# GpSimd's waits for the VectorE operation planned ahead of it, taken out of a retention and SwiGLU kernel

## The chip, the core and the metric

The kernel runs on one core of a Trainium2 chip. The metric is the device time of one execution in microseconds (us); of several executions the median counts. The engines are TensorE (PE, with its weight loads as PEld), VectorE (DVE), ScalarE (ACT), GpSimd (POOL) and SyncE (SP), which issues nearly all DMAs.

## What is computed

A retention layer (linear attention with a decay per head) over 4 sequences of 768 positions and 8 heads of 64, in blocks of 64, and behind it an RMS norm and a SwiGLU layer with 512 inputs and 1536 hidden columns:

```python
for b in range(nb):                       # retention, block by block
    intra = einsum('bhic,bhjc->bhij', qb, kb) * Dmask
    intra = einsum('bhij,bhjd->bhid', intra, vb)
    inter = einsum('bhid,bhde->bhie', qb * lam_pow, kv_state)
    out[:, :, sl] = intra + inter
    kv_state = lam_block * kv_state + einsum('bhsd,bhse->bhde', kb * rev_pow, vb)
...
xn = x / sqrt(mean(x * x) + 1e-06) * rms_g   # x: the layer's rows, 3072 x 512
g, val = xn @ w_gate, xn @ w_val
return (silu(g) * val) @ w_out
```

## The kernel before

The 3072 rows are worked on in 6 groups of 512 (m), the hidden columns in 12 blocks of 128 (f). A unit is a group and a block: gate and value products, SiLU, their product. Each float32 operand is split into a high and a low float16 part, and a product is made of three float16 products. The first 24 units (groups 0 and 1) use the weights as they are (`classical`, matmuls at L668 with 512 columns). The others use a scheme of seven half-size products in place of eight (`strassen`, L779 with 256 columns), which needs sums of blocks of the weights and of the rows. The retention of a later group is done between units, a pair of heads at a time (`Pair`): scores (L477), the decayed scores (`decay_a`, L497), the states (L510, L523, L525), the mix (L538, L549), squares for the norm (L572, added up at L578, and over the partitions at L589). The rows of the result are made at L938 for group 0 and at L1050 for the others.

GpSimd does 102 tensor operations: the decay of q (`decay_q`, L501), sums of squares (`add_squares`, L578), the power for the norm (`root`, L612), low parts of the normed rows (L644), of their sums (`low_sums`, L663) and of the weights' sums (`low`, L729), and the sum of a weight's high and low part (`whole`, L708). VectorE does the same kinds of work on other tiles, and besides: conversion of the weights' bits (L216, L219), their low parts (L440), sums of the weights (L717 to L721) and of the output weights (L269 to L275), the unit's sums and products (L837, L845, L857, L866), the low parts of the operands of the last product (L922, L1013).

The order of the work is made by a planner (`Plan`). Each step has an engine, a cost, a due time, what it reads and writes and the buffers it opens; `Plan.run` (L1154) simulates the engines and sets the order. `SHIFTS`, a table, moves due times of single steps. The planner holds that GpSimd and some VectorE steps exclude each other: `shared(i)` (L1150) is true for every GpSimd step and for the VectorE steps named in `SHARED` (L1096), and `run` lets neither start before the other's last one is 0.13 us from its end (L1191, L1237).

The loop behind `order = plan.run()` (L1958) writes the steps down in the planned order. Each engine carries out its own instructions in that order, and waits on semaphores where data or buffers ask for it. The planned turn between the two engines is no such reason. So the loop adds one: after a shared VectorE step, the next GpSimd step gets a wait for that step's last instruction. VectorE gets no wait for GpSimd.

Of the kernel before, what the change touches and what calls it, by code (L numbers as in the profile page):

```python
# [22 lines left out]
def retention_swiglu_kernel(  # L23
# [11 lines left out]
    nc = tc.nc  # L35
# [1221 lines left out]
    plan = Plan()  # L1257
# [241 lines left out]
    def arrive_steps():  # L1499
        def arrive():  # L1500
            pass

        step("LD", 4.3, -9, arrive, w=["cs", "come"])
        times = [0.75, 1.3, 1.55, 1.35, 1.85, 1.3, 1.3, 1.3]
        for p in range(NP):
            for i, c in enumerate(("qK", "kv")):
                step("LD", times[2 * p + i], -9, arrive, w=["come", *[f"q0_{p}:{x}" for x in c]])
        step("LD", 3.05, -9, arrive, w=["come", "gv0"])

    def ramp_steps():  # L1510
        pm = []

        def largest_of_all():
            pm.append(scales())

        def make_scales():
            scales_of(pm[0])

        step("DVE", 0.13, -3.1, largest, r=["cs"], w=["gmax"])
        step("PE", 0.3, -3.1, largest_of_all, r=["gmax"], w=["pmax"], new=[("pmax", "g")])  # L1520
        step("DVE", 1.33, -2.35, make_scales, r=["pmax"], w=["gs"])
        for p in range(NP):
            for part in range(3):
                w = f"pw{p}" if part == 2 else f"mask{2 * p + part}"
                step("DVE", 0.38, -3.2 + 0.4 * p + 0.15 * (part == 2), powers, p, part, r=["cs"] + ["wv11"] * (part == 2), w=[w])
        ats = [-2.85, -2.3, -2.0, -1.75]
        pairs = [Pair(0, p) for p in range(NP)]
        for q, at in zip(pairs, ats):
            pair_scores(q, at)
            pair_sums(q, at + 0.4)  # L1530
            pair_mix(q, at + 0.5)
        first_norm_steps(0, -0.3, 0.05)
        for p, at in enumerate(ATTENTION_1):
            q = Pair(1, p)
            pair_scores(q, at)
            pair_sums(q, at + 0.5)
            pair_mix(q, at + 0.6)
        first_norm_steps(1, 5.0, 0.05)
        for f, at in enumerate(CONVERT):
            wt = Weights(f)  # L1540
            if wt.halves:
                for i in range(2):
                    halved_steps(wt, at + 0.2 * i, i)
            else:
                convert_steps(wt, at)
                split_steps(wt, at + 0.35)
# [196 lines left out]
    def load_steps():  # L1743
        queue = [(1, 0), (1, 1), (1, 2), 1, (1, 3), *range(2, NF)]
        queue += [(m, p) for m in range(2, NG) for p in range(NP)]
        for n, key in enumerate(queue):
            cost = 2.65 if n < 5 else 3.0 if n < 10 else 3.6
            lasts = (0.1, 0.1, 0.5, 0.4)[n] if n < 4 else 2.3
            if isinstance(key, tuple):
                m, p = key  # L1750
                if key == (3, 1):
                    step("LD", 0.0, -9, operand_tiles, new=[("tx0", "in"), ("tx1", "in")],
                         w=[f"{t}:{o}{i}" for t in ("tx0", "tx1") for o in "hl" for i in range(2)]
                         + [f"vals{i}:{j}" for i in range(2) for j in range(2)])
                name = f"q{m}_{p}"
                step("LD", cost, -9, load_qkv, m, p, w=[f"{name}:{c}" for c in "qKkv"], new=[(name, "in")], lasts=lasts)
            else:
                step("LD", cost, -9, load_gv, key, w=[f"gv{key}"], new=[(f"gv{key}", "in")], lasts=lasts)
# [123 lines left out]
    with tc.manual_schedule(  # L1882
        engines={
            mybir.EngineType.PE, mybir.EngineType.DVE, mybir.EngineType.Activation,
            mybir.EngineType.Pool, mybir.EngineType.SP,
        }
    ):
        hs = {u: Hidden(u, m, f) for u, (m, f) in enumerate(units)}
        columns = {u: [] for u in range(2 * NF)}
        arrive_steps()  # L1890
        load_steps()
        ramp_steps()
        out_weights = [out_weight_steps(j, at) for j, at in enumerate(OUT_W)]
        end = len(units)
        pair = None
        for u in range(end):
            for f in COLUMNS.get(u, []):
                columns[u + 1].append(column_steps(f, u - 0.7))
            if u == FACTORS:
                factor_steps(u)  # L1900
            for f in range(NF):
                if int(SUMS[f]) == u:
                    sum_steps(f, SUMS[f])
            h = hs[u]
            m, f = h.m, h.f
            if u < 2 * NF:
                classical(u, h, columns[u])
                n = u - (2 * NF - 8)
                if 0 <= n < NP:
                    q = Pair(2, n)  # L1910
                    pair_scores(q, u + 0.62)
                    pair_sums(q, u + 0.64)
                    if pair:
                        pair_mix(pair, u + 0.63)
                    pair = q
                elif n == NP:
                    pair_mix(pair, u + 0.63)
                elif n == NP + 1:
                    norm_steps(2, u, 0.11)
                if u == 2 * NF - 1:  # L1920
                    pair = Pair(3, 0)
                    pair_scores(pair, u + 0.62)
            else:
                strassen(u, h)
                p = (f + 1) // 2 % HALF
                following = m + 2 if f == NF - 1 else m + 1
                if f % 2 == 0 and pair:
                    pair_sums(pair, u + 0.12)
                    pair_mix(pair, u + 0.3)
                    pair = None  # L1930
                if f % 2 and p < NP and following < NG:
                    pair = Pair(following, p)
                    pair_scores(pair, u + 0.1)
                if f == 2 * NP - 1 and m + 1 < NG:
                    norm_steps(m + 1, u, 0.2)
        if PLAIN:
            step("ROOM", 0.0, START[0] - 3, early_room, new=[("early", "big0")], w=["early:"])
        for m in range(PLAIN):
            for j in range(HALF):
                block_steps(m, j, START[m] - 1.5 - 0.3 * (HALF - 1 - j), 0.1)  # L1940
            plain_rows_steps(m, START[m], PLAIN_LENGTH)
        for o, at in zip(out_weights, OUT_SUMS):
            out_sum_steps(o, at)
        for i in range(2):
            room_step(i, START[PLAIN] - 3)
        for m, at in enumerate(START):
            if m < PLAIN:
                continue
            for j in range(HALF):
                t = at - AHEAD[j]  # L1950
                if m == NG - 1:
                    t = units.index((NG - 1, 2 * j + 1)) + 0.5
                operand_steps(m, j, t, 0.1)
            rows_steps(m, at, LENGTH)
        for i, by in SHIFTS.items():
            eng, cost, at, *rest = plan.steps[i]
            plan.steps[i] = (eng, cost, at + by, *rest)
        order = plan.run()  # L1958
        now, gaps = 1.5, True
        traced, ahead = nc.cur_bb.bb.instructions, None  # L1960
        for t, i in order:
            eng, cost, _, fn, args, _, _, new, _ = plan.steps[i]
            begun = len(traced)
            if eng == "PE":
                if any(name.startswith("pb") for name, _ in new):
                    gaps = False
                idle = t - now
                if gaps and idle > 0.8:
                    busy(int((idle - 0.5) / 0.24))
                now = t + cost  # L1970
            fn(*args)
            if plan.shared(i):

                engine = mybir.EngineType.Pool if eng == "POOL" else mybir.EngineType.DVE
                mine = [x for x in traced[begun:] if x.engine == engine]
                if eng == "DVE":
                    ahead = mine[-1].name
                elif ahead:
                    tc.add_manual_dep(
                        mine[0], ahead,  # L1980
                        mybir.DependencyInfo(mybir.DependencyClass.Sync, mybir.DependencyReason.DATA),
                        reason="shared port",
                    )
                    ahead = None

# [63 lines left out]
```

## Time and profile before

| | |
|---|---|
| median of 3 runs | 629.96 us (629.2 to 631.78) |
| the profiled execution | 629.99 us |
| its span, first to last instruction | 628.2 us |
| granted TensorE clock | 1.000 of full speed |
| busy: PE, DVE, ACT, POOL | 622.2, 452.8, 383.9, 127.6 us |
| GpSimd instructions | 113 |

A row of the profile names a line of the kernel, an engine, an operation, what it writes and reads, and times. The end of a matmul is modelled, so that TensorE's busy time says less than the pace of its matmuls. Idle time of an engine is put down to what released the instruction behind it; of several waits that is the one that came last.

### The profile page before, as it was taken

The page shows a single profiled execution, that of the slowest core. Times are in us where ns is not written, and L with a number is a line of the kernel's source. Part 1 is how long each engine was busy: PE and PEld are TensorE (multiplying, and loading weights), DVE is VectorE, ACT ScalarE, POOL GpSimd, SP SyncE. Part 2 cuts the span into 40 slices and gives each one's busy share as a digit, 9 for nine tenths or more (in the row PEclk, how much of TensorE's full clock was granted, in tenths as well). Part 3 has the DMA queues.
Part 4 walks back from the last instruction along what each step waited for, and adds up shares of the span by engine and source line. Part 5 has one row for each costly group of instructions (what it writes and reads, how often), then busy time and mean ns, then how long its engine had stood idle before and what let it go on. Part 6 is the DMA issues. An engine that isn't in the chain of part 4 may idle for free.

```text
span 628.2 us, 14174 instructions
## 1 busy us (share of the span) xinstructions
PE 622.2 (99%) x5665; PEld 479.3 (76%) x5665; DVE 452.8 (72%) x886; ACT 383.9 (61%) x724; POOL 127.6 (20%) x113
## 2 busy tenths in 40 slices
PE   9999999999999999999999999999999999999997
PEld 8864444455657777668888888888889888888886
DVE  6889888777787778788875789634874778546641
ACT  3779799986546764568764685534853564445531
POOL 3531201142825665410020110011000110000000
DMA  8899898888646788878878667744675667343401
GB/s 320 305 318 299 313 313 290 288 279 290 231 148 226 258 284 273 275 265 284 269 268 297 216 212 225 244 179 152 226 224 179 202 207 248 109 135 105 148 18 51
DMA packets 56033, 144.05 MB, mean 229 GB/s; under 512 B 5920, under 2 KB 18208, under 8 KB 54560
## 3 DMA queue, kind: packets, MB, share of 16 engines
q1 hardware_dynamic: 55824, 142.64, 67.3%
q8 instruction: 44, 0.72, 0.5%
q10 hardware_dynamic: 144, 0.52, 0.3%
q14 instruction: 21, 0.17, 0.1%
HBM read 106.96 MB, written 36.18 MB: 228 GB/s over the span
## 4 chain that ended last, share of the span: by engine, by line
PE 94%; DMA 2%; DVE 1%; ACT 1%; SPq 0%; issue 0%; POOL 0%; ACTq 0%; POOLq 0%
PE o L1050 20%; PE pa L779 20%; PE pb L779 15%; PE pv L668 9%; PE pg L668 9%; PE o L938 5%; PE pa L477 4%; PE po L538 3%; PE po L549 3%; DMA qkv<-in_qkv_dram 2%; PE o_own L1050 2%; PE pst L510 2%; PE pss L589 1%; PE unread L144 1%; PE pr L630 0%
## 5 line engine op out<-in xcount | busy, mean ns | idle before, releaser
L779 PEld LDWEIGHTS <-gw 128*128 128x128 f16 x1440 | 139.5, 98 | 21.9 <-issue 0.8
L1050 PE MATMUL o<-wo,late 128*128 128x256 f16 x1152 | 143.9, 273 | 0.5 <-ACT late L1061 0.5
L1050 PEld LDWEIGHTS <-late 128*128 128x128 f16 x1260 | 123.0, 98 | 15.1 <-issue 0.8
L668 PEld LDWEIGHTS <-w_half 128*128 128x128 f16 x576 | 53.9, 98 | 60.5 <-issue 1.5
L833 ACT COPY tx<-pa 128x256 f32<-128x256 f32 x96 | 35.3, 371 | 72.9 <-PE pa L779 55.5
L779 PE MATMUL pa<-tx,gw 128*128 128x256 f16 x576 | 77.4, 273 | 0.0
L668 PE MATMUL pv<-x,w_half 128*128 128x512 f16 x288 | 69.2, 379 | 0.2
L668 PE MATMUL pg<-x,w_half 128*128 128x512 f16 x288 | 66.8, 379 | 0.0
L837 DVE TENSOR_TENSOR tx<-pb,tx 128x256 f32<-128x256 f32 x96 | 40.0, 420 | 31.4 <-PE pb L779 29.1
L779 PEld LDWEIGHTS <-gv 128*128 128x128 f16 x576 | 56.0, 98 | 7.4 <-issue 0.2
L501 POOL TENSOR_TENSOR qkv<-qkv,pw 128x512 f32<-128x512 f32 x24 | 30.6, 1275 | 74.8 <-PE pa L477 66.5
L845 DVE TENSOR_TENSOR sg<-pb,sg 128x256 f32<-128x256 f32 x48 | 20.1, 422 | 35.4 <-ACT sg L841 30.7
L1013 DVE TENSOR_TENSOR late<-s,late 128x1024 f16<-128x1024 f32 x30 | 37.3, 1253 | 5.2 <-ACT late L1009 5.1
L708 POOL TENSOR_TENSOR r<-w_half 128x512 f32<-128x512 f16 x24 | 27.7, 1163 | 63.3 <-DVE w_half L440 25.5
L497 DVE TENSOR_TENSOR a<-pa,mask 128x512 f32<-128x512 f32 x48 | 31.4, 683 | 12.0 <-PE pa L477 8.5
L779 PE MATMUL pa<-x,gv 128*128 128x256 f16 x288 | 39.3, 273 | 0.0
L779 PE MATMUL pb<-x,gv 128*128 128x256 f16 x288 | 39.3, 273 | 0.0
L779 PE MATMUL pa<-x,gw 128*128 128x256 f16 x288 | 39.0, 273 | 0.0
L779 PE MATMUL pb<-tx,gw 128*128 128x256 f16 x288 | 39.0, 273 | 0.0
L779 PE MATMUL pb<-x,gw 128*128 128x256 f16 x288 | 38.7, 273 | 0.0
L938 PE MATMUL o<-wo,early 128*128 128x512 f16 x144 | 34.9, 379 | 0.0
L729 POOL TENSOR_TENSOR ws<-ws,ws 128x512 f16<-128x512 f32 x24 | 28.8, 1210 | 29.3 <-DVE en L325 15.3
(152 smaller groups left out, 1031.0 us busy)
## 6 DMA issues: line engine op xcount, KB each, us to landing
gw<-gw_kept SPq DMA_DIRECT2D x48, 640.0 KB, 4.8
qkv<-in_qkv_dram SPq DMA_DIRECT2D x47, 512.0 KB, 6.0
h<-h_kept SPq DMA_DIRECT2D x30, 512.0 KB, 4.1
h_kept<-sg SPq DMA_DIRECT2D x48, 256.0 KB, 3.4
gv<-gw_kept SPq DMA_DIRECT2D x48, 256.0 KB, 4.4
raw_gv<-in_weights_dram SPq DMA_DIRECT2D x11, 1024.0 KB, 7.2
raw_o<-in_weights_dram SPq DMA_DIRECT2D x24, 256.0 KB, 4.4
gw_kept<-ws SPq DMA_DIRECT2D x12, 512.0 KB, 4.2
```

The lines of the kernel that those rows point to most:

```text
L477: nc.tensor.matmul(self.pa[j][:, c, :], self.kT[r, c, :], self.qT[r, c, :], start=True, stop=True,)
L497: nc.vector.tensor_mul(self.a[:, j], self.pa[j], decay)
L501: eng.tensor_mul(self.qT, self.qT, pw[:, p : p + 1, :].broadcast_to([P, GC, P]))
L668: nc.tensor.matmul(ps, w[:, kk, :], x[:, kk, :], start=i == kk == 0, stop=i == 2 and kk == NK - 1,)
L708: nc.gpsimd.tensor_add(self.r[:, i], w[:, 0], w[:, 1])
L729: eng.tensor_sub(self.to[:, c, 1], self.t[:, c], self.to[:, c, 0])
L779: nc.tensor.matmul(ps, w(ow, k), x(ox, k), start=first and i == k == 0, stop=i == 2 and k == 1, skip_group_check=True,)
L833: nc.scalar.copy(self.val_sums[:, self.half(t)], self.pa)
L837: nc.vector.tensor_add(v, self.pb, v)
L938: nc.tensor.matmul(self.banks[t], h[:, oh, t * P : (t + 1) * P], wo[:, j, 3 + 2 * k : 5 + 2 * k, ow], start=j == k == i == 0, stop=j == HA ...
L1013: eng.tensor_sub(lo, of, hi)
L1050: nc.tensor.matmul(bank[:, t], ops[:, oh, t * P : (t + 1) * P], w[:, ow], start=n in (1, 2, 5) and q == i == 0 and (t == 0 or bank is own) ...
```

## The change

The loop no longer adds the waits. The planner is as it was, so the order of every engine's instructions is the same.

```diff
         now, gaps = 1.5, True
-        traced, ahead = nc.cur_bb.bb.instructions, None
         for t, i in order:
             eng, cost, _, fn, args, _, _, new, _ = plan.steps[i]
-            begun = len(traced)
...
             fn(*args)
-            if plan.shared(i):
-
-                engine = mybir.EngineType.Pool if eng == "POOL" else mybir.EngineType.DVE
-                mine = [x for x in traced[begun:] if x.engine == engine]
-                if eng == "DVE":
-                    ahead = mine[-1].name
-                elif ahead:
-                    tc.add_manual_dep(
-                        mine[0], ahead,
-                        mybir.DependencyInfo(mybir.DependencyClass.Sync, mybir.DependencyReason.DATA),
-                        reason="shared port",
-                    )
-                    ahead = None
```

No instruction moves. What differs are GpSimd's waits, here around 229 us of the profile: the sums of the high and low parts of weights 10 and 11 (`r`, two halves each, L708), the low parts of the sums of weight 8 (`ws_8`, L729) and the power for the norm of group 3 (`y`). The numbers in names are those of buffers; DVE_49, PE_49 and so on are the engines' semaphores.

```order
 L708 TENSOR_TENSOR r_2892<-w_half_96 128x512 [waits DVE_49,Pool_49]
 L729 TENSOR_TENSOR ws_8_2894<-ws_2863,ws_8_2894 128x2x256 [waits DMAHW4_49,DMAHW6_49,DMAHW0_49,Activation_49]
-L729 TENSOR_TENSOR ws_8_2894<-ws_2863,ws_8_2894 128x2x256 [waits DVE_49]
-L708 TENSOR_TENSOR r_2892<-w_half_96 128x512 [waits DVE_49]
-L708 TENSOR_TENSOR r_2960<-w_half_96 128x512 [waits PE_49]
-L708 TENSOR_TENSOR r_2960<-w_half_96 128x512 [waits DVE_49]
+L729 TENSOR_TENSOR ws_8_2894<-ws_2863,ws_8_2894 128x2x256
+L708 TENSOR_TENSOR r_2892<-w_half_96 128x512
+L708 TENSOR_TENSOR r_2960<-w_half_96 128x512 [waits DVE_49,PE_49]
+L708 TENSOR_TENSOR r_2960<-w_half_96 128x512
 L612 TENSOR_TENSOR y_3012<-ms_2969,power 128x4 [waits DVE_49]
```

Three operations in a row lose their wait for VectorE; the first of `r_2960` now names VectorE because the wait that held it implicitly, that of the operation ahead of it, is gone.

## Rows read from the trace of the kernel before

**Rows 1.** The page: busy time of each engine, and the shares of the chain of work that ended last.
```profile
PE 622.2 (99%) x5665; PEld 479.3 (76%) x5665; DVE 452.8 (72%) x886; ACT 383.9 (61%) x724; POOL 127.6 (20%) x113
PE 94%; DMA 2%; DVE 1%; ACT 1%; SPq 0%; issue 0%; POOL 0%; ACTq 0%; POOLq 0%
```
**Rows 2.** Who waited for whom, TensorE alone, all entries: us in total, times, longest us.
```profile
PE unread L144 <- POOL ident masks.py:199: 1.5, 1, 1.5
PE pss L589 <- POOL sq L578: 0.5, 1, 0.5
PE o L1050 <- ACT late L1061: 0.5, 1, 0.5
```
**Rows 3.** The chain that ended last, in order of time: start us, us, what.
```profile
50.49 1.13 DVE w L219
52.34 1.04 PE pv L668 x4
...
114.15 6.91 PE pg L668 x32
...
358.61 5.24 PE o L1050 x48
```
**Rows 4.** Who waited for whom, GpSimd, four entries: us in total, times, longest us.
```profile
POOL tx L663 <- DVE t L275: 5.8, 1, 5.8
...
POOL tx L663 <- DVE ws L721: 4.4, 1, 4.4
...
POOL sq L578 <- DVE ws L721: 3.4, 1, 3.4
...
POOL qkv L501 <- DVE pw L158: 2.8, 1, 2.8
```
**Rows 5.** Instructions in order of time, VectorE around 213 us: start us, us, engine, line, operation, out<-in, shapes, count, [idle before <- what ended it]. Rows of one shape are merged with their count.
```profile
213.25 0.42 DVE L720 TENSOR_TENSOR ws<-r,ws 128x256 f32<-128x256 f32 x1
213.71 1.26 DVE L721 TENSOR_TENSOR ws<-r,ws 128x256 f32<-128x256 f32 x1
215.08 1.29 DVE L497 TENSOR_TENSOR a<-pa,mask 128x512 f32<-128x512 f32 x2
```
**Rows 6.** The same view of GpSimd.
```profile
213.37 1.32 POOL L708 TENSOR_TENSOR r<-w_half 128x512 f32<-128x512 f16 x1 [0.76 <-DVE ws L718]
215.05 1.15 POOL L708 TENSOR_TENSOR r<-w_half 128x512 f32<-128x512 f16 x1 [0.36 <-DVE ws L721]
```
**Rows 7.** The same view around 60 us, GpSimd and VectorE.
```profile
60.32 1.50 POOL L612 TENSOR_TENSOR y<-ms,power 128x4 f32<-128x4 f32 x1 [11.38 <-DVE sc L430]
...
61.09 0.69 DVE L216 TENSOR_SCALAR w<-w 128x1024 int32<-128x1024 int32 x1 [0.72 <-ACT w L209]
```
**Rows 8.** The same view around 40 us: GpSimd, ScalarE, VectorE, TensorE.
```profile
40.82 1.27 POOL L578 TENSOR_TENSOR sq<-sq,sq 128x512 f32<-128x512 f32 x1 [4.38 <-DVE e L426]
...
39.18 0.60 ACT L572 ACTIVATE sq<-po 128x512 f32<-128x512 f32 x1
...
41.34 0.61 ACT L416 ACTIVATE junk<-w 128x512 bf16<-128x512 f32 x1
...
39.51 0.42 DVE L216 TENSOR_SCALAR w<-w 128x512 int32<-128x512 int32 x1
39.96 0.69 DVE L219 SCALAR_TENSOR_TENSOR w<-raw_gv,w 128x512 int32<-128x512 int32 x1
...
42.10 0.16 PE L420 MATMUL pn<-ssq,ones_b 128*128 128x1 bf16 x1
```
**Rows 9.** The same view around 47 us: TensorE, GpSimd, VectorE.
```profile
44.97 1.16 PE L477 MATMUL pa<-qkv 64*128 64x128 f32 x16
...
47.66 1.28 POOL L501 TENSOR_TENSOR qkv<-qkv,pw 128x512 f32<-128x512 f32 x1 [4.34 <-DVE w_half L440]
...
46.78 0.75 DVE L440 SCALAR_TENSOR_TENSOR w_half<-w,sc,w_half 128x512 f16<-128x512 f32 x1 [0.75 <-ACT w_half L436]
...
48.05 1.44 DVE L219 SCALAR_TENSOR_TENSOR wo_f<-raw_o,wo_f 128x512 int32<-128x512 int32 x1
```
**Rows 10.** The same view around 230 us: GpSimd, VectorE, TensorE.
```profile
228.70 1.16 POOL L729 TENSOR_TENSOR ws<-ws,ws 128x512 f16<-128x512 f32 x1 [0.63 <-DVE sg L857]
231.00 2.26 POOL L708 TENSOR_TENSOR r<-w_half 128x512 f32<-128x512 f16 x2 [1.14 <-DVE sq L578]
...
230.22 0.69 DVE L578 TENSOR_TENSOR sq<-sq,sq 128x512 f32<-128x512 f32 x1 [0.76 <-POOL ws L729]
...
231.03 1.00 PE L589 MATMUL pss<-ones,sq 128*128 128x1 f32 x8
```
**Rows 11.** The same view around 355 us: ScalarE, GpSimd, VectorE, TensorE.
```profile
353.52 0.83 ACT L659 CAST tx<-xt 128x768 f16<-128x768 f32 x1 [0.53 <-DVE xt L655]
...
355.42 1.64 POOL L663 TENSOR_TENSOR tx<-xt,tx 128x768 f16<-128x768 f32 x1 [5.30 <-DVE sg L857]
...
354.53 0.75 DVE L857 SCALAR_TENSOR_TENSOR sg<-tx,cg,sg 128x512 f32<-128x512 f32 x1
355.19 0.68 DVE L497 TENSOR_TENSOR a<-pa,mask 128x512 f32<-128x512 f32 x1
...
357.09 0.42 DVE L845 TENSOR_TENSOR sg<-pb,sg 128x256 f32<-128x256 f32 x1 [0.56 <-ACT sg L841]
...
357.80 0.71 PE L779 MATMUL pb<-x,gw 128*128 128x256 f16 x5
```

## The prediction

> **What bounds the kernel now.** The page comes first: TensorE is busy for 622.2 us of a span of 628.2 us, and the chain that ended last lies on it for 94% [rows 1]. Because ends of matmuls are modelled, the chain is read next for their pace: 32 matmuls of 512 columns take 6.91 us, 216 ns each, and 48 of 256 columns take 5.24 us, 109 ns each [rows 3]. They follow one another with nothing between. The table of TensorE's waits has three entries of 2.5 us together, and only one of them, 0.5 us, is a wait for GpSimd [rows 2]. So the change can win little, since TensorE has almost nothing to give back. It can lose: any operation that VectorE delivers later than TensorE needs it adds to the end.
>
> The last view to read is how GpSimd and VectorE treat each other. Around 213 us, VectorE's L720 and L721 have the same shape and both inputs in SBUF. L720 takes 0.42 us, L721 takes 1.26 us [rows 5]. GpSimd's operation began at 213.37 and ended at 214.69 [rows 6]; L721 ended at 214.97. L721 stood still until GpSimd was done, and then needed 0.28 us: of its own 0.42 us, 0.14 us had passed before it met the obstacle. The reverse stands in the same rows. GpSimd's 213.37 operation took 1.32 us and the same one at 215.05 took 1.15 us: it waited 0.17 us for the end of L720 (213.67), and took its turn before L721, which was issued at 213.71. L497, which reads one of its inputs from PSUM, ran beside GpSimd at 215.08: two in 1.29 us, as fast as one in 0.68 us elsewhere [rows 5, 11]. So the two engines exclude each other for operations with two SBUF inputs, and whoever reaches the obstacle first goes first. A late VectorE operation is late by GpSimd's end, less its own start, less 0.14 us.
>
> **The change part by part.** The orders on all engines are the same; 49 of GpSimd's 102 tensor operations lose VectorE from their list of waits and others keep only an older VectorE operation, whose result they read. No instruction, byte or queue position is added. Nothing else gets a new wait in any stage: the few waits that appear on ScalarE and SyncE stand for results that those steps needed before too.
>
> Where VectorE is in the middle of the awaited operation when GpSimd's data are ready, the semaphore is exchanged for the exclusion and GpSimd starts some 0.1 us sooner. Such places cost nothing and gain nothing; TensorE's one 0.5 us wait for GpSimd has ScalarE in front of it. What counts are places where the data are ready before VectorE starts the operation that GpSimd had to let pass. There VectorE pays.
>
> First, 39.8 us [rows 8]. The squares that GpSimd's L578 adds are there at 39.78, and it would run from 39.83 to 41.10 instead of from 40.82. VectorE's L219 (39.96) is late by 41.10 - 39.96 - 0.14 = 1.0 us and ends at 41.65. ScalarE's L416 reads that weight, so it moves from 41.34 to 41.7, and TensorE's L420 at 42.10, which follows L416 by 0.15 us in which the sum is read out, stands for 0.35 us. Most of it comes back: at 47 us the scores end at 46.13 [rows 9], GpSimd's L501 goes at 46.5 instead of 47.66, VectorE's L440 (46.78) is late by 0.9 us, but L219 (48.05, 1.44 us instead of 0.69) no longer stands. Behind it VectorE is late by 0.15 us only. It is VectorE that TensorE waits for at 52.34, as the chain has it [rows 3], so 0.15 us is left of the 0.35. I take 0.15.
>
> Second, 231 us [rows 10]. GpSimd's row sum L708 for weight 10 needs nothing that isn't long there; it would follow the operation of 228.70 at 229.8 and end at 230.95. VectorE's L578 (230.22) is late by 230.95 - 230.22 - 0.14 = 0.6 us and ends at 231.5. TensorE's L589 at 231.03 waits for just that, with 0.12 us to spare: 0.5 us are lost.
>
> Third, 354 us [rows 11]. ScalarE's half is there at 354.35, so L663 would run from 354.40 to 356.04. VectorE's L857 (354.53) is late by 356.04 - 354.53 - 0.14 = 1.4 us. What follows on VectorE moves with it up to L845, which had 0.56 us of idle time before it: it starts 1.4 - 0.6 = 0.8 us late and ends at 358.3 instead of 357.51. TensorE's matmul at 357.80 overwrites the bank that L845 reads and had 0.28 us to spare: 0.5 us are lost.
>
> Four more places have this shape, each named by a wait that ends with VectorE [rows 4]: L501 behind the scan of line 158, L663 behind L721, L578 behind L721, L663 behind L275. The three places above bound each between 0 and 0.5 us. Without a look at what TensorE has to spare at each, I take 0.2 us, a little under the middle: 0.8 us. The other removed waits I take at nothing: VectorE's idle time behind them covers them, and where that cover is gone each would cost up to 0.5 us as well. A gain is bounded by the 2.5 us of [rows 2]; I take none.
>
> Sum: 0.15 + 0.5 + 0.5 + 0.8 = 2.0 us on the profiled execution's 629.99 us, which equals the median of the runs shown (629.96): **632.0 us**.
>
> **A rule beside a row.** GpSimd's L612 began at 60.32 and ran for 1.50 us; VectorE's L216, issued at 61.09, ran its plain 0.69 us to 61.78, and L612 ended 0.04 us behind it [rows 7]. The earlier start did not give L612 the ports; it took them only when it had something to move. The Trainium skill (SBUF — State Buffer, Who interferes with whom) says that the operation issued first holds the shared pair for the whole instruction and the other fully blocks. The row speaks against "whole" for this operation; the rows around 213 us agree with the rest. By the rule as written the sum would be up to 1 us higher, since L612 would go ahead of small VectorE operations at 60 us; it is among the rivals.
>
> **The rivals.** *Nothing arrives at TensorE.* VectorE's gaps take up all seven delays, as they take up L721's 0.84 us now: 630.0 us. For it speaks that TensorE shows only 2.5 us of waits in a kernel in which VectorE is already held up often; against it, the 0.12 and 0.28 us of slack read above. 17%.
>
> *GpSimd runs in a row and shuts VectorE out.* At 229.8 us three L708 (two for weight 10 and 11 in [rows 10], and a second for 11) would stand ready one behind the other, held back by L578 and L857 until now. If the next GpSimd operation takes the ports ahead of a waiting VectorE operation, L578 waits for all three: 229.8 + 3 x 1.15 = 233.25, late by 2.9 us, so TensorE loses 2.8 us there instead of 0.5: 634.3 us, slower than before. It decides from the moment that a second GpSimd operation is ready when the first ends. Against it: a GpSimd operation also passes some 0.13 us before it needs the ports (213.37 to 213.67 is 0.30 us, of which it lost 0.17), in which a waiting VectorE operation can go. No row shows the meeting itself. 15%.
>
> *L612 holds the ports from its start*, the rule above: VectorE's small operations at 60 us are up to 1 us late and TensorE pays 0 to 1 of it: 632.0 to 633.0 us. [Rows 7] speak against it. 5%.
>
> *Faster*: earlier GpSimd results release TensorE. All of TensorE's waits together are 2.5 us, so 627.5 us is the end of that. 3%.
>
> That the change doesn't do what it says is no rival: the waits are gone from the built program.
>
> **How the numbers follow.** The forecast has 60%, with 631.0 to 633.4 us as its own range (the four small places at 0 or at 0.4 each). A measurement of this kernel can tell about 0.5% from no change, 3.15 us. Above 633.1 us lie a sixth of the forecast (10%), nearly all of the runs in a row (13%) and some of the third rival (2%): slower 25%. Faster is the last rival, 3%. The rest, 72%, is within 0.5%. The range reaches down through the case that nothing arrives, with the 0.7 us by which the runs before lie under their median, and up past the runs in a row: 629.3 to 634.8 us.
>
> **What would show it.** L219 at 40 us, L578 at 230 us and L857 at 354 us must show 1.0, 0.6 and 1.4 us more than their plain time, and TensorE a gap just behind each: new entries for VectorE in the table of TensorE's waits. GpSimd's waits for VectorE must shrink to those for data. If VectorE's long operations are there but TensorE has no gaps, the second case holds. If L578 takes over 2 us, the third does. The prediction is wrong if the time falls under 629 us, or if TensorE loses time where VectorE was not held up.

## The result, and the profile after

| | median (us) | ratio to the kernel before, 95% interval |
|---|---|---|
| before, 6 runs | 631.48 (629.2 to 632.12) | |
| after, 6 runs | 637.75 (634.62 to 639.36) | 1.0096 [1.0074, 1.0118] |
| after, 6 runs on another occasion | 636.71 (636.06 to 638.22) | 1.0068 [1.0053, 1.0084], before at 631.79 |

The change makes the kernel slower by 0.7 to 1.0%, 4 to 6 us. The forecast was 2.0 us more, 632.0 us, and its range ended at 634.8 us.

The page of the kernel after: busy times, and the shares of the chain that ended last. They answer to [rows 1].

```profile
PE 624.8 (98%) x5665; PEld 480.0 (75%) x5665; DVE 462.9 (73%) x886; ACT 383.8 (60%) x724; POOL 132.6 (21%) x113
...
PE 84%; DVE 7%; DMA 4%; ACT 2%; issue 1%; SPq 1%; POOL 0%; ACTq 0%; DVEq 0%; POOLq 0%
```

VectorE does the same 886 instructions in 10.1 us more, GpSimd its 113 in 5.0 us more: no instruction was added, so this is time in which one stands for the other. VectorE's share of the chain went from 1% to 7%.

TensorE's table of waits (us in total, times, longest), which answers to [rows 2]:

```profile
PE pa L779 <- ACT sg L841: 1.7, 1, 1.7
...
PE po L538 <- DVE a L497: 1.4, 2, 1.2
PE o L1050 <- ACT late L1061: 1.1, 1, 1.1
PE pss L589 <- DVE sq L578: 0.9, 1, 0.9
...
PE pb L779 <- DVE sg L845: 0.3, 1, 0.3
```

VectorE has new entries, as forecast, and the two largest, L538 and L589, stand at places that the forecast did not price at this size. The first entry is chance: the second profile of the same kernel has nothing there. In this one L841 waited for a store of h that took 6.8 us instead of 4.2.

The chain that ended last (start us, us, what) has VectorE's L578 ahead of the L589 entry:

```profile
174.04 1.47 DVE sq L578
175.56 1.05 PE pss L589 x8
```

Ahead of that L578 stand four additions of 128x256, one behind the other, and each takes over twice its plain 0.42 us [rows 5]. Why, the rows in order of time say, VectorE and GpSimd around 169 us (start us, us, engine, line, operation, out<-in, shapes, count, [idle before <- what ended it]):

```profile
167.50 1.03 DVE L717 TENSOR_TENSOR ws<-r 128x256 f32<-128x256 f32 x1
168.46 1.49 DVE L718 TENSOR_TENSOR ws<-r 128x256 f32<-128x256 f32 x1
169.98 1.38 DVE L720 TENSOR_TENSOR ws<-r,ws 128x256 f32<-128x256 f32 x1
171.39 1.26 DVE L721 TENSOR_TENSOR ws<-r,ws 128x256 f32<-128x256 f32 x1
...
168.21 1.46 POOL L578 TENSOR_TENSOR sq<-sq,sq 128x512 f32<-128x512 f32 x1
169.62 1.45 POOL L501 TENSOR_TENSOR qkv<-qkv,pw 128x512 f32<-128x512 f32 x1
171.03 1.33 POOL L708 TENSOR_TENSOR r<-w_half 128x512 f32<-128x512 f16 x1
```

L718 stands until GpSimd's L578 ends at 169.67 and is done 0.28 us later, at 169.95. GpSimd's L501 began at 169.62, ahead of L720 (169.98). It takes 1.45 us in place of 1.27, since it waits for the rest of L718; L720 then stands until L501 ends at 171.07. L721 meets L708 in the same way. The two engines **take turns**, one operation each. In the kernel before, GpSimd's L501 waited here until L721 was through:

```profile
165.38 0.91 DVE L717 TENSOR_TENSOR ws<-r 128x256 f32<-128x256 f32 x1
166.21 0.41 DVE L718 TENSOR_TENSOR ws<-r 128x256 f32<-128x256 f32 x1
166.66 0.43 DVE L720 TENSOR_TENSOR ws<-r,ws 128x256 f32<-128x256 f32 x1
167.12 1.38 DVE L721 TENSOR_TENSOR ws<-r,ws 128x256 f32<-128x256 f32 x1
...
168.63 1.28 POOL L501 TENSOR_TENSOR qkv<-qkv,pw 128x512 f32<-128x512 f32 x1 [0.41 <-DVE ws L721]
```

So two of the four additions stood with the waits in, too. The change takes the row from two meetings to four, from 3.13 to 5.16 us in sum.

The same around 216 us, VectorE, GpSimd and TensorE, answering to [rows 5, 6]:

```profile
214.06 1.50 DVE L721 TENSOR_TENSOR ws<-r,ws 128x256 f32<-128x256 f32 x1
...
216.14 0.99 DVE L717 TENSOR_TENSOR ws<-r 128x256 f32<-128x256 f32 x1
217.06 1.37 DVE L718 TENSOR_TENSOR ws<-r 128x256 f32<-128x256 f32 x1
218.47 1.37 DVE L720 TENSOR_TENSOR ws<-r,ws 128x256 f32<-128x256 f32 x1
219.87 0.42 DVE L721 TENSOR_TENSOR ws<-r,ws 128x256 f32<-128x256 f32 x1
...
214.00 1.27 POOL L578 TENSOR_TENSOR sq<-sq,sq 128x512 f32<-128x512 f32 x1 [3.78 <-ACT sq L572]
215.69 2.45 POOL L708 TENSOR_TENSOR r<-w_half 128x512 f32<-128x512 f16 x2 [0.42 <-DVE ws L721]
218.11 1.45 POOL L501 TENSOR_TENSOR qkv<-qkv,pw 128x512 f32<-128x512 f32 x1
...
221.15 0.43 PE L538 MATMUL po<-a,qkv 128*64 128x128 f32 x2 [1.25 <-DVE a L497]
```

The first L721 belongs to the sums of weight 7, the others to those of weight 6. In the kernel before, two of these five stood: L717 here and the L721 of [rows 5] (1.26 us).

```profile
210.77 0.42 DVE L721 TENSOR_TENSOR ws<-r,ws 128x256 f32<-128x256 f32 x1
...
211.78 1.11 DVE L717 TENSOR_TENSOR ws<-r 128x256 f32<-128x256 f32 x1
212.81 0.41 DVE L718 TENSOR_TENSOR ws<-r 128x256 f32<-128x256 f32 x1
```

Again two meetings became four, and the five additions take 5.65 us in sum in place of 3.62.

The places that the forecast priced, 40 us [rows 8], 231 us [rows 10] and 355 us [rows 11] of the kernel before, in the kernel after:

```profile
40.79 1.78 DVE L219 SCALAR_TENSOR_TENSOR w<-raw_gv,w 128x512 int32<-128x512 int32 x1
...
40.75 1.27 POOL L578 TENSOR_TENSOR sq<-sq,sq 128x512 f32<-128x512 f32 x1 [3.48 <-DMA qkv<-in_qkv_dram]
...
235.49 0.97 DVE L578 TENSOR_TENSOR sq<-sq,sq 128x512 f32<-128x512 f32 x1 [0.76 <-ACT sq L572]
...
234.76 3.82 POOL L708 TENSOR_TENSOR r<-w_half 128x512 f32<-128x512 f16 x3
...
362.82 2.08 DVE L857 SCALAR_TENSOR_TENSOR sg<-tx,cg,sg 128x512 f32<-128x512 f32 x1
...
362.72 1.64 POOL L663 TENSOR_TENSOR tx<-xt,tx 128x768 f16<-128x768 f32 x1 [4.31 <-ACT tx L659]
...
366.55 0.70 PE L779 MATMUL pb<-x,gw 128*128 128x256 f16 x5 [0.29 <-DVE sg L845]
```

L219 is late by 1.78 - 0.69 = 1.09 us (forecast 1.0), L857 by 2.08 - 0.75 = 1.33 us (1.4), L578 by 0.28 us (0.6).

Since the order of the instructions is the same in both kernels, each of TensorE's 5665 matmuls can be compared with itself: its start in one trace less its start in the trace of before is TensorE's lateness. The table gives how much it grows in each stage, in us; a stage is named by its times in the profile of before. The last two columns are the sum and the timed ratio.

| | 0-40 | 40-60 | 60-100 | 100-165 | 165-200 | 200-225 | 225-245 | 245-262 | 262-300 | 300-345 | 345-370 | to end | sum | ratio |
|---|---|---|---|---|---|---|---|---|---|---|---|---|---|---|
| before, second profile | -0.11 | 0.26 | 0.95 | 0.00 | 0.00 | 0.00 | 0.00 | 0.01 | 0.00 | 0.68 | 0.00 | 0.29 | 2.1 | |
| after | 0.83 | 0.90 | -0.15 | 0.55 | 1.16 | 1.98 | 0.23 | 2.20 | 0.00 | 0.59 | 0.45 | 0.02 | 8.8 | 1.0096 |
| after, second profile | 2.04 | 0.60 | -0.16 | 0.65 | 1.17 | 1.97 | 0.23 | 0.00 | 0.32 | 0.25 | 0.46 | 0.00 | 7.5 | 1.0068 |
| runs_only | 0.24 | 0.18 | -0.15 | 0.00 | 0.61 | 1.98 | 0.00 | 0.00 | 0.00 | -0.28 | 0.00 | 0.00 | 2.6 | 1.0039 |
| all_but_runs | -0.45 | 0.35 | 0.29 | 0.89 | 0.00 | 0.01 | 0.42 | 0.00 | 0.00 | 0.45 | 0.46 | 0.00 | 2.4 | 1.0026 |
| priced_only | -0.09 | 0.25 | 0.36 | 0.14 | 0.00 | 0.39 | 0.56 | 0.04 | 0.41 | 0.11 | 0.46 | 0.27 | 2.9 | 1.0040 |
| keep_two | 0.23 | 0.17 | 1.25 | 0.49 | 0.00 | 0.12 | 0.46 | 0.00 | 0.29 | 0.72 | 0.45 | 0.28 | 4.5 | 1.0058 |
| keep_ten | 1.94 | 0.68 | 0.27 | 0.17 | 0.00 | 0.13 | 0.62 | 0.56 | 0.00 | -0.06 | 0.00 | 0.00 | 4.3 | 1.0023 |
| keep_thirteen | 0.03 | 0.99 | 0.74 | 0.23 | 0.00 | 0.37 | -0.04 | 0.00 | 0.00 | 0.53 | 0.00 | 0.15 | 3.0 | 1.0019 |
| short_pool | -0.33 | 0.72 | 1.04 | 1.00 | 0.00 | -0.01 | 0.08 | 1.23 | 0.00 | 0.91 | 0.46 | 0.33 | 5.4 | 1.0050 |
| halves | 1.11 | 0.30 | -0.16 | 1.00 | 0.00 | 0.62 | 0.34 | 0.00 | 1.06 | 0.97 | 0.46 | 0.15 | 5.8 | 1.0068 |

Six stages move by themselves: the three before 100 us, 300 to 345 and the end (up to 0.95 us between two profiles of the kernel before), and 245 to 262 (2.20 and 0.00 us in the two profiles of the kernel after). The other six, the steady ones, stand still to 0.01 us in the kernel before, and both profiles of the kernel after agree in them to 0.1 us, but for 262 to 300. In these six the kernel after loses 4.4 us in one profile and 4.8 us in the other, 3.1 of it between 165 and 225 us.

### The profile page after: what moved, and what is told of

It reads as the page before. It is cut to its first block, busy times and chain, and to the rows that moved or that the text cites. A ratio compares the mean times of both kernels' runs of the same rounds, so it can differ in the third digit from the quotient of the medians.

```text
span 637.0 us, 14156 instructions
## 1 busy us (share of the span) xinstructions
PE 624.8 (98%) x5665; PEld 480.0 (75%) x5665; DVE 462.9 (73%) x886; ACT 383.8 (60%) x724; POOL 132.6 (21%) x113
## 4 chain that ended last, share of the span: by engine, by line
PE 84%; DVE 7%; DMA 4%; ACT 2%; issue 1%; SPq 1%; POOL 0%; ACTq 0%; DVEq 0%; POOLq 0%
PE o L1050 19%; PE pa L779 18%; PE pb L779 14%; PE pg L668 8%; PE pv L668 8%; PE o L938 4%; PE pa L477 3%; PE po L538 2%; PE po L549 2%; PE o_own L1050 2%; PE pst L510 1%; DMA qkv<-in_qkv_dram 1%; DMA raw_gv<-in_weights_dram 1%; DMA h_kept<-sg 1%; PE pss L589 1%
## 5 line engine op out<-in xcount | busy, mean ns | idle before, releaser
L501 POOL TENSOR_TENSOR qkv<-qkv,pw 128x512 f32<-128x512 f32 x24 | 31.4, 1310 | 75.5 <-PE pa L477 75.5
L708 POOL TENSOR_TENSOR r<-w_half 128x512 f32<-128x512 f16 x24 | 29.5, 1244 | 61.3 <-DVE ws L721 37.6
L497 DVE TENSOR_TENSOR a<-pa,mask 128x512 f32<-128x512 f32 x48 | 31.3, 682 | 13.5 <-PE pa L477 9.9
L729 POOL TENSOR_TENSOR ws<-ws,ws 128x512 f16<-128x512 f32 x24 | 29.5, 1243 | 35.2 <-ACT ws L725 35.2
L841 ACT COPY sg<-pa 128x256 f32<-128x256 f32 x48 | 17.9, 372 | 30.2 <-PE pa L779 23.1
```

What stands on the lines that cost most here:

```text
L497: nc.vector.tensor_mul(self.a[:, j], self.pa[j], decay)
L501: eng.tensor_mul(self.qT, self.qT, pw[:, p : p + 1, :].broadcast_to([P, GC, P]))
L708: nc.gpsimd.tensor_add(self.r[:, i], w[:, 0], w[:, 1])
L729: eng.tensor_sub(self.to[:, c, 1], self.t[:, c], self.to[:, c, 0])
```

## The experiments

The first theory is that of **runs**: where several VectorE operations follow one another and several GpSimd operations are ready, each of VectorE's stands for one of GpSimd's, and the delays add up. The rival is the prediction's own arithmetic, one delay per place. The kernels keep or take out single waits; GpSimd's steps are counted from 0 in the planned order. The edit of runs_only, against the kernel before:

```diff
-        traced, ahead = nc.cur_bb.bb.instructions, None
+        traced, ahead, turn = nc.cur_bb.bb.instructions, None, -1
+        TAKEN_OUT = {41, 42, 43, 44, 57, 58, 59, 60, 61}
...
             if plan.shared(i):
+                turn += eng == "POOL"
...
                 elif ahead:
-                    tc.add_manual_dep(
+                    if turn not in TAKEN_OUT:
+                        tc.add_manual_dep(
```

**after_again** is the changed kernel itself, without an edit.

> The changed kernel once more, for a second profile. Theory R (runs): where VectorE has several short operations with two SBUF inputs in a row, and GpSimd several operations ready, the two now take turns, and every VectorE operation of the row stands for one GpSimd operation (1.37 to 1.49 us instead of 0.42); the delays add up. Then TensorE's gaps must come back at the same places: about 1.0 us before the row sums L589 of group 2 (174 us), 1.4 us before L538 at 219.5 us and 0.5 us more around it. Theory D (a transfer by chance): the gap of 1.9 us before L779 at 258 us stood behind a store of h that took 6.8 us instead of 4.2, and need not come back. Time by both about 637 us.

636.71 us, 1.0068 [1.0053, 1.0084]. The gaps between 165 and 225 us came back at the same places, to 0.01 us (third row of the table); the 2.2 us between 245 and 262 us did not. So that stage is a transfer's chance, and the gaps that came back are the change.

**before_again** is the kernel before, without an edit.

> The kernel before once more, for a second profile: how far TensorE's lateness moves by itself between two executions of one program. Both theories: shifts of up to 0.9 us in the first 40 us, where data arrive, and at single later places of up to 0.6 us that come and go (behind transfers), but nothing of 1 us or more before L589 of group 2 or before L538 of pair 3_2, where both profiles of the changed kernel show 1.06 and 1.07, and 1.6 and 1.6 us.

632.07 us, one run. Lateness moved by 0.95 us between 60 and 100 us, 0.68 us between 300 and 345 us, and by no more than 0.01 us in the steady stages.

**runs_only**, **all_but_runs** and **priced_only** take out the waits at nine steps (the diff above), everywhere but at those nine (`if turn in KEPT` with the same set), and at the prediction's places:

```diff
+        TAKEN_OUT = {1, 13, 14, 15, 49, 57, 68, 84, 92}
```

> The waits are taken out at nine GpSimd steps alone: the four around the sums of weight 2 (166 to 172 us) and the five around those of weights 7 and 6 (211 to 219 us). Theory R: VectorE alternates with GpSimd there as in the changed kernel, L718, L720 and L721 of weight 2 and L717 to L720 of weight 6 take about 1.4 us each; TensorE loses about 1.0 us before L589 and 1.4 to 1.9 us around 219 us: 2.4 to 2.9 us over the kernel before. Theory P (as predicted, one delay per place, at most 0.5 us of it at TensorE): 0.2 to 1.0 us over it.

634.32 us, 1.0039 [1.0021, 1.0057]: about 2.5 us from 9 steps. The trace has 0.61 us at weight 2 and 1.98 us at weight 6, the theory's size at the second place and six tenths of it at the first, where L718 met nothing (0.41 us) and three of the four additions stood.

> The complement of the run with nine steps at 166 to 172 us and 211 to 219 us: the waits stay at those nine steps and are taken out everywhere else. Theory R: the gaps before L589 at 174 us and around 219 us are gone, 2.4 to 2.9 us less than the changed kernel, some 3.5 us over the kernel before. Theory P: at most 1.0 us less than the changed kernel, 5 us or more over the kernel before.

634.04 us, 1.0026 [1.0011, 1.0040]: 1.6 us over the kernel before, less than half of the 3.5 us expected; both stages are gone from the trace. The two ratios add up to 1.0065, the changed kernel on the same chip had 1.0068.

> The waits are taken out at nine GpSimd steps alone: those at 40, 42 and 47 us, L708 at 231 us, L663 at 355 us, and the four with the longest waits (L501 behind the scan of line 158, L663 behind L721, L578 behind L721, L663 behind L275). Theory P: the sum of the prediction, 2.0 us over the kernel before. Theory R: no queue of ready GpSimd operations arises, since the step behind each of these still has its wait; only the gaps that the changed kernel showed at 42.7 and 48.0 us (0.5 and 0.4 us), 236 us (0.2) and 366 us (0.5) are there: 1.0 to 1.6 us, and nothing at 219 us.

634.92 us, 1.0040 [1.0024, 1.0056]: 2.5 us, which fits the prediction's 2.0. It lies above the 1.0 to 1.6 of the theory of runs, which expected nothing at 219 us, though the interval begins at 1.5 us. The trace has 0.25 us at 40 to 60 us, 0.39 at 200 to 225, 0.56 at 231, 0.41 at 273 and 0.46 at 355. VectorE's rows at two of the places, 211 and 231 us:

```profile
211.45 1.50 DVE L721 TENSOR_TENSOR ws<-r,ws 128x256 f32<-128x256 f32 x1
...
213.86 0.41 DVE L718 TENSOR_TENSOR ws<-r 128x256 f32<-128x256 f32 x1
214.31 0.42 DVE L720 TENSOR_TENSOR ws<-r,ws 128x256 f32<-128x256 f32 x1
...
231.28 1.29 DVE L578 TENSOR_TENSOR sq<-sq,sq 128x512 f32<-128x512 f32 x1 [0.76 <-POOL ws L729]
```

L578 is late by 1.29 - 0.69 = 0.60 us, as forecast, and L721 by 1.07 us, which costs TensorE 0.39 us; L718 and L720 behind it are plain, because the next GpSimd steps still wait. With the wait at 211 us taken out alone, the stage loses 0.39 us; with those of the steps behind it taken out too (runs_only), 1.98 us.

**keep_two** is the changed kernel with two waits, at one step in each of the two rows:

```diff
+        KEPT = {42, 59}
```

> The changed kernel with two of the waits kept, those of L501 at the sums of weight 2 and of the second L708 of weight 8 at the sums of weight 6: GpSimd stands at one point in each of the two rows. Theory R: from there VectorE's row runs free (L720 and L721 of weight 2, and L718, L720 and L721 of weight 6, about 0.43 us each in place of 1.3 to 1.4), the gaps before L589 at 174 us and L538 at 219 us fall under 0.3 us: 2.4 to 2.7 us under the changed kernel, some 2.3 us over the kernel before. If each removed wait costs its own delay and no more, two waits bring back at most 1.0 us.

635.12 us, 1.0058 [1.0037, 1.0078]. In the trace the two stages fall from 1.16 and 1.98 us to 0.00 and 0.12. VectorE at weight 6:

```profile
215.91 0.41 DVE L718 TENSOR_TENSOR ws<-r 128x256 f32<-128x256 f32 x1
216.36 0.42 DVE L720 TENSOR_TENSOR ws<-r,ws 128x256 f32<-128x256 f32 x1
```

The medians do not show the 2.4 us: the interval overlaps that of after_again. The profiled execution lost 1.25 us between 60 and 100 us, a stage that moves by itself. What the two waits are worth is shown by the trace alone.

**short_pool** leaves all waits out and takes the meeting away: four GpSimd operations (steps 41, 42, 57, 60) have 8 columns in place of 512. The kernel leaves out most of the sums of squares and of the decay of q there.

```diff
-            eng.tensor_add(sums[0], sums[0], s1)
+            n = 2 if short[0] else P
+            eng.tensor_add(sums[0][:, :, :n], sums[0][:, :, :n], s1[:, :, :n])
...
+            short[0] = eng == "POOL" and turn in {41, 42, 57, 60}
```

> The changed kernel, all waits out, with four GpSimd operations cut to 8 columns (what they leave out: most of the sum of squares at 168 and 214 us, L578, and most of the decay of q at 170 and 218 us, L501). The orders and the other steps stay. Theory R (the price is the meeting, not the missing wait): VectorE's L718 and L720 of weight 2, L721 of weight 7 and L720 of weight 6 meet nothing and take about 0.43 us; TensorE's gaps before L589 at 174 us (1.06) and before L538 at 219 us (1.6) fall under 0.3 us together or nearly so: about 2.5 us under the changed kernel, some 2.5 to 3.5 us over the kernel before. Rival: the waits keep something else in step (buffers, the queue of SyncE); then the gaps stay, though GpSimd has less to do.

634.95 us, 1.0050 [1.0030, 1.0070]: 3.2 us over the kernel before. The two stages are at 0.00 and -0.01 us with no wait kept. GpSimd and VectorE at weight 2 (the lines lie 4 further down):

```profile
168.76 0.42 DVE L722 TENSOR_TENSOR ws<-r 128x256 f32<-128x256 f32 x1
169.21 0.42 DVE L724 TENSOR_TENSOR ws<-r,ws 128x256 f32<-128x256 f32 x1
...
168.51 0.39 POOL L582 TENSOR_TENSOR sq<-sq,sq 128x8 f32<-128x8 f32 x1
```

So it is the meeting that costs, not the missing wait as such.

**turns** and **turns2** measure the meeting by itself; the rest of the computation is left out. Eight VectorE operations stand beside GpSimd operations of several sizes; the lines are those of turns2.

```diff
+    for work in (both, held_in_psum, shift):
+        for n, size in ((1, 8), (4, 512), (8, 256), (2, 1024)):
+            begin()
+            gpsimd(n, size)
+            work(8)
```

> The meeting by itself, nothing else of the computation. Sections: VectorE alone, 8 additions of 128x256 float32 with both inputs in SBUF; GpSimd alone, 4 additions in the form of L708 (128x512); both together; the same with GpSimd's in 8 pieces of 256 columns, then in 2 of 1024; VectorE's with one input in PSUM; last VectorE's integer shift with a single input in SBUF (the operation of L216). Theory R: beside 4 GpSimd operations of 512 columns, 4 of VectorE's 8 take about 1.4 us, turn by turn, and the others 0.42; beside 8 pieces, 8 of them take about 0.8; beside 2 of 1024, two take about 2.5. VectorE's sum grows by about the same 4 us in all three: GpSimd's whole time while VectorE has work. With a PSUM input 0.42 us each and no turns. The prediction held that two SBUF inputs are what excludes: by that the shift runs beside GpSimd without delay; the changed kernel's L216 at 124 us (1.38 us in place of 0.42) says that it doesn't, and takes turns too. A rival: GpSimd's next ready operation goes ahead of the waiting one on VectorE; then one VectorE operation takes 4 us or more.

Its sections overlapped: the shifts ran ahead of all GpSimd work and the additions with an input in PSUM behind it, so those two parts showed nothing. In the rest, seven additions in a row took 1.25 to 1.42 us each beside seven GpSimd operations of 512 columns, 0.77 to 0.90 beside 256, 2.1 to 2.2 beside 1024: turns, and no operation that stood for two.

> The meeting by itself again, each section now begun behind the end of the one ahead; nothing else of the computation. VectorE does 8 operations a section: additions with both inputs in SBUF (L57), additions with one input in PSUM (L61), shifts with a single input in SBUF (L65, the operation of L216); beside them GpSimd does nothing to speak of (128x8), 4 additions of 512 columns, 8 of 256, 2 of 1024. Theory R: both in SBUF: 4 of 8 at 1.25 us beside the four, 8 of 8 at 0.77 beside the eight, 2 at 2.2 beside the two, else 0.42, as in the first such run where the sections overlapped. One input in PSUM: 0.42 throughout, GpSimd at its plain 1.15. Single input in SBUF: turns, as for two (the changed kernel's L216 shows 1.38 us at 124 us). By the prediction's rule (two SBUF inputs) the shift would show no turns.

VectorE's sections in turns2 (us runs from the start of the first of eight operations to the end of the last). L57 has both inputs in SBUF, L61 one in PSUM, L65 is the shift with a single input. Of each line's four sections, the first is beside next to nothing (one GpSimd operation of 8 columns), the others beside four GpSimd operations of 512 columns, eight of 256, two of 1024:

```profile
7.29 3.64 DVE L57 TENSOR_TENSOR dve<-a,go 128x256 f32<-128x256 f32 x8 [3.73 <-ACT a L49]
11.53 6.96 DVE L57 TENSOR_TENSOR dve<-a,go 128x256 f32<-128x256 f32 x8 [0.60 <-ACT a L49]
19.09 5.73 DVE L57 TENSOR_TENSOR dve<-a,go 128x256 f32<-128x256 f32 x8 [0.60 <-ACT a L49]
26.35 7.23 DVE L57 TENSOR_TENSOR dve<-a,go 128x256 f32<-128x256 f32 x8 [1.53 <-ACT a L49]
...
39.22 3.63 DVE L61 TENSOR_TENSOR dve<-held,a 128x256 f32<-128x256 f32 x8 [1.00 <-ACT held L52]
...
56.89 3.65 DVE L65 TENSOR_SCALAR dvi<-ints 128x512 int32<-128x512 int32 x8 [1.52 <-ACT ints L51]
...
61.69 6.97 DVE L65 TENSOR_SCALAR dvi<-ints 128x512 int32<-128x512 int32 x8 [0.94 <-ACT ints L51]
```

GpSimd's sections of four operations, beside L57 and beside L61:

```profile
12.17 5.12 POOL L70 TENSOR_TENSOR gps<-half 128x512 f32<-128x512 f16 x4 [3.94 <-ACT half L53]
...
39.45 4.84 POOL L70 TENSOR_TENSOR gps<-half 128x512 f32<-128x512 f16 x4 [4.43 <-ACT half L53]
```

Four operations of 512 columns cost VectorE 6.96 - 3.64 = 3.32 us, 0.83 each; two of 1024 cost 3.59 us, 1.80 each; of the eight of 256, six met one (single operations of 0.77 in place of 0.42 us) and cost 2.09 us, 0.35 each. GpSimd pays little: 5.12 in place of 4.84 us for four. With an input in PSUM the additions take 3.63 us beside four operations of 512 columns, so there they pay nothing. The shift with one SBUF input pays as the additions do.

**keep_ten** and **keep_thirteen** keep the first GpSimd step ahead of each place where the lateness grew, and then three more:

```diff
+        KEPT = {13, 15, 23, 34, 42, 57, 59, 68, 84, 92}
```

```diff
+        KEPT = {13, 14, 15, 23, 34, 42, 57, 59, 67, 68, 77, 84, 92}
```

> The changed kernel with ten of its waits kept, the first GpSimd step ahead of each place where TensorE's lateness grew in both profiles of it (42, 48, 124, 160, 172, 216, 231, 273 and 358 us). Theory R: these are all that count; no more than 0.6 us over the kernel before. If the other 39 removed waits cost something that no gap shows, 1 us or more over it.

632.73 us, 1.0023 [1.0005, 1.0042], 1.4 us where at most 0.6 was expected. At 231 us 0.62 us stayed, although the wait of L708 there was kept: GpSimd's L729 ahead of it had lost its own and held up L857, which VectorE does ahead of L578.

> The kernel with ten waits kept, and three more: the second L501 at 42 us, the second L729 of weight 8 at 229 us (in the kernel with ten, VectorE's L857 met it, took 1.39 us for 0.75, and L578 behind it came late: 0.6 us at TensorE) and L708 at 247 us. The other 36 of the removed waits stay out. Theory R: the step at 231 us is gone too (under 0.2 us); 0 to 1.0 us over the kernel before. If the step at 231 us stays at 0.4 to 0.6 us, it has another cause than GpSimd's earlier start.

632.75 us, 1.0019 [1.0004, 1.0035], 1.2 us, somewhat more than expected. The step at 231 us is gone (-0.04). Thirteen waits bring back most of the cost; of the 1.2 us the steady stages of the trace show 0.56 (0.23 at 160 us, 0.37 at 200 to 225, -0.04 at 231), the rest is not placed.

**halves** keeps no wait and writes most long GpSimd operations as two of 256 columns, for instance:

```diff
-            nc.gpsimd.tensor_add(self.r[:, i], w[:, 0], w[:, 1])
+            for j in range(2):
+                c = slice(j * HG, (j + 1) * HG)
+                nc.gpsimd.tensor_add(self.r[:, i, c], w[:, 0, c], w[:, 1, c])
```

> The changed kernel, all waits out, with nearly every long GpSimd operation of 512 columns (L501, L578, L708, L729) written as two of 256. By the meeting measured by itself a VectorE operation then pays 0.35 us for each turn in place of 0.83, and a row of four beside a queue of GpSimd operations 1.4 us in place of 3.3; GpSimd's own work grows by some 5 us, which nobody waits for. Theory R: TensorE's gaps before L589 at 174 us (1.06 us) and L538 at 219 us (1.6 us) fall under 0.3 us each without any wait; 2 us or more under the changed kernel, 1 to 3 us over the kernel before. Rival: what counts is GpSimd's whole time in the queue, not the length of one operation; then VectorE meets twice as many, and the gaps stay at 1 us or more.

635.80 us, 1.0068 [1.0049, 1.0086], no better than the changed kernel: the expected time was missed, and the 5 us more on GpSimd were 23.2 (155.8 us against 132.6). turns2 could have told: beside L61 eight operations of 256 columns take 5.89 us and four of 512 take 4.84, 0.26 us more for each one split, and 84 were split. At the two places it did what was expected of VectorE, and TensorE's gaps were 0.00 us and, over the 0.3 us expected, 0.62 us. VectorE at weight 6 (L727 and L729 are L718 and L720):

```profile
215.39 0.89 DVE L727 TENSOR_TENSOR ws<-r 128x256 f32<-128x256 f32 x1
216.31 0.77 DVE L729 TENSOR_TENSOR ws<-r,ws 128x256 f32<-128x256 f32 x1
```

But GpSimd's operations reached other rows: at 273 us L275 took 0.83 us in place of 0.43 and TensorE lost 1.06 us, at 132 us two L440 took 2.33 us in place of 1.57 and TensorE lost 0.79 us in place of 0.20. The cost moved.

## Why the prediction was wrong

**What bounds the kernel**, and that the change can hardly win: right. TensorE's two largest gaps in the steady stages end with VectorE (L578, L497). One reading was wrong: two of the three entries of [rows 2] are waits for GpSimd, 2.0 of the 2.5 us. The 1.5 us are for the identity matrix at the start (L144), so the sum doesn't change.

**The delay of one meeting** (GpSimd's end, less VectorE's start, less 0.14 us): right in size. L219 1.09 us for 1.0, L857 1.33 us for 1.4, L578 0.60 us for 0.6 with only the priced waits out (0.28 us in the changed kernel).

**The three priced places**: 40 and 47 us, 0.15 us forecast. In priced_only L420 at 42.10 starts 0.37 us later (0.35 forecast) and 0.20 us comes back at 52.34, as forecast, though not by the meeting it named: L440 kept its 0.75 us there. The rest of that stage's 0.25 us moves in the kernel before too. In the changed kernel L420 loses 0.50 and 0.32 us in the two profiles, and nothing comes back. 231 us, 0.5 us forecast, 0.56 us in priced_only; 0.23 us in the changed kernel, where L708 began earlier, 0.73 us ahead of L578 (0.41 us in priced_only), and held it for less. 354 us, 0.5 us forecast, 0.45 to 0.46 us in every trace with that wait out.

**Four more places at 0.2 us**: the sum of 0.8 came out in priced_only, by luck: 0.39 us for L578 behind L721, 0.41 for L663 behind L275, nothing visible for the other two. In the changed kernel's two profiles L663 behind L275 shows 0.00 and 0.32 us. These places at 0 or 0.4 us each give 631.1 to 632.7 us, not the 631.0 to 633.4 that the forecast names as its own range.

**"The other removed waits I take at nothing: VectorE's idle time behind them covers them"**: this is the step that failed. The waits of neighbouring steps were priced one by one, as if the others stayed; where the others do stay (priced_only) that arithmetic holds. With all of them out, GpSimd has a queue of ready operations, and the waits of L578 and L501 beside the sums of weight 2, taken at nothing, make three meetings in a row (1.49, 1.38, 1.26 us) where there was one (1.38 us): 1.16 us at TensorE. L578 behind L721, priced at 0.2 us, is the first of four meetings with the L708 and L501 behind it, where there were two: 1.98 us. VectorE has no idle time inside such a row; each of the two rows ends 2.03 us later on VectorE's side. These two and the 0.55 to 0.65 us between 100 and 165 us are 3.7 to 3.8 us of the 4.4 to 4.8 us; the prediction had 0.2 us for them. Of the gaps between 100 and 165 us, at 124, 132 and 160 us, none was tested apart; at 124 us VectorE's L216 meets GpSimd's L729 and takes 1.38 us in place of 0.42.

**The rivals**: GpSimd does run in a row (three L708 at 234.76 us, without idle time), but it does not shut VectorE out: L578 went between the first and the second and took 0.97 us, and no addition in turns2 stood for two. Its price of 2.9 us at 231 us was wrong, its hint that a queue of ready operations is what matters was right. That L612 holds the ports from its start is out: in the changed kernel VectorE's L922, with two inputs in SBUF, began at 239.39 us beside an L612 that ran from 238.54 to 240.00, and took its plain 1.21 us. That nothing arrives, and a gain, are out by the time.

**Exclusion by two SBUF inputs** was too narrow: the shift of L65 has one, and pays the same. The Trainium skill (SBUF — State Buffer, Who interferes with whom) lists this kind of operation (`tensor_scalar`) among those that can contend; the trace agrees (6.97 us in place of 3.65). VectorE's conversions of the output weights between 120 and 155 us consist of this operation, L216, and of L219.

**The size.** The steady stages hold 4.4 us in the profile of the runs that lost 6.0 us [4.7, 7.4], and 4.8 us in that of the runs that lost 4.3 us [3.3, 5.3]. What remains in the first isn't placed. The base moved too: the three runs that the forecast started from had a median of 629.96 us, the six had 631.48, and 1.5 us of the distance between 632.0 and 637.75 us is that.

## What to carry to other kernels

A wait that only keeps two engines apart is priced with its neighbours: find the longest row of operations on the engine that matters, count the operations that would stand ready on the other one, charge one meeting for each pair, and take off the meetings that are there already with the waits in (two in each row here). Behind the first of a row, a meeting cost VectorE GpSimd's operation less some 0.3 us. In the trace, one kept wait in the middle of each of the two rows did the work of all of that row's waits (0.00 and 0.12 us left); the time of that kernel doesn't show it.

## What the runs showed of the hardware

Where VectorE had additions with two inputs in SBUF or shifts ready and GpSimd had additions, the two took turns in turns2, one operation each, as long as both had work. Back to back, a VectorE operation pays the other's length less 0.32 us (0.35 of 0.67, 0.83 of 1.15, 1.80 of 2.12 us), as an addition with two inputs in SBUF and, beside 512 columns, as a shift with one (6.97 against 3.65 us for eight); GpSimd pays 0.07 us a turn (5.12 against 4.84 us for four). An addition with an input in PSUM pays nothing (3.63 us beside any of them). GpSimd's L612 (128x4) was an exception: VectorE's L216 [rows 7] and L922, each begun behind it, took their plain 0.69 and 1.21 us. The two profiles of the changed kernel agree on the steady gaps to 0.1 us, but for the one at 273 us, and most of them to 0.01 us, while its runs spread by 2 to 5 us; so the trace told experiments apart that the medians could not.
